# k by heads in 1 KB runs, v of the first two batches without its column of ones, q of the second batch in 768 B runs

## The chip, the cores and the metric

The kernel is one program on one core of a Trainium2 chip. A core has five engines with their own instruction streams: PE (TensorE, matrix products into eight PSUM banks; its weight loads are listed as PEld), DVE (VectorE), ACT (ScalarE), POOL (GpSimd) and SP (SyncE, which here only issues DMAs). Each works through its own list in order and waits on semaphores for the others. The metric is the device time of one execution in microseconds; of several executions the median is taken.

## The reference

```python
B, H, S, D = 8, 8, 576, 64                      # float32 q, k, v
q_s = exp(q - max(q, axis=-1));  q_s /= sum(q_s, axis=-1) + 1e-09     # over the 64 columns of a row
k_s = exp(k - max(k, axis=2));   k_s /= sum(k_s, axis=2) + 1e-09      # over the 576 rows of a head
kv  = einsum('bhsd,bhse->bhde', k_s, v)         # 64x64 per batch and head
att = einsum('bhsd,bhde->bhse', q_s, kv)        # -> x: 4608 tokens x 512
h   = x @ w_in                                  # 512 -> 2048, float64 weights
out = (h / (1 + exp(-1.702 * h)) @ w_out)       # 2048 -> 512, float32
```

The attention is linear: per batch and head a 64x64 matrix kv is built from k and v, and the softmaxed q is multiplied by it. Then comes a two-layer feed-forward network. The two weight matrices arrive as float64, 8.4 MB each; the kernel splits each into a high and a low float32 half, so that three products (high by high, high by low, low by high) stand for one.

## The kernel before, in words

The 4608 tokens are cut into 12 blocks t of 384 (a partition holds three neighbouring rows, C = 3). A batch has 576 rows, so block 0 lies in batch 0 and block 1 spans batches 0 and 1. The 2048 hidden columns are cut into 16 pieces j of 128. For every pair (t, j) there is `g1` (12 matmuls 128x384 on line 593: for each of four 128-row chunks c of x the products wh by xh, wh by xl, wl by xh), the gelu on ACT (`gt`), its high half on ACT (`gh`) and its low half on DVE (`gl`, line 605), and `g2` (three parts of three matmuls 128x512, line 625: gh by wh, gh by wl, gl by wh).

Weights are loaded once. `load_w` brings 512 KB of raw float64 per piece; `conv_w` makes the two halves in place: c1 on ACT (line 248), c2 on DVE (line 252), c3 on DVE (lines 256 and 257), c5 on ACT (line 261, the high half) and c6 on DVE (line 267, the low half). The word "wi3" below is the piece j = 3 of `w_in`, "wo3" of `w_out`.

The attention of the first two batches is done in groups of four heads (`group`), from buffers that sit in the memory which the late weights take over afterwards (`early`, with a tag per weight tile). k comes in 512 of its 576 rows (four neighbouring rows, CM = 4, per partition) and a tail of 64 rows (`load_tail`). Per group of four heads the steps are

- `k_max`: three maxima on DVE (lines 390 to 392), then a maximum over the partitions on POOL;
- `k_sub`: subtraction on DVE (lines 414, 417), exponential on ACT (lines 420, 421); of batch 0 the result goes to a second buffer `em` with the heads inside the chunks;
- `q_soft`: row maxima and subtraction on DVE (lines 493, 494), exponential on ACT (line 497), sums, reciprocals and the scaling on DVE (lines 500 to 503);
- `kv_pairs`, per pair of heads: for each of five row chunks and two heads one matmul (line 456) with k as the 64-column weights and v as the moving operand. v has a 65th column of ones, so the same matmul also gives the sum of k's exponentials; DVE turns that column into reciprocals r (lines 461, 462) and ACT scales with it (line 472);
- `q_tr`, three transposes per pair of heads on PE (line 520), copied to SBUF on ACT; `x_pairs`, the product with kv (lines 563, 568); and `x_out`, its high half xh on ACT (line 535) and low half xl on DVE (line 538).

Batches from 2 on go through the buffers kt, vt and qt in groups of two heads.

The order on every engine is set ahead of time: each step is put into `Plan` with an engine, an assumed cost, what it reads and writes, and a rank. `Plan.order` plays the steps through with these assumed costs, takes on each free engine the ready step of lowest rank, and so fixes the five lists. A load counts with a landing time worked out from its `size` at 270 KB/us. An engine keeps its list even if at run time a later step were ready first. Changing an assumed cost or a buffer therefore reorders lists far from the line that changed.

## Time and profile before

| | us |
|---|---|
| median of 3 runs (lowest, highest) | 917.77 (916.34, 918.44) |
| the profiled execution | 914.53 |
| its span, first to last instruction | 912.8 |
| PE busy in it | 880.8 |

A row of the timeline or of the chain of waits starts with a time from the span's start and a duration. The merged rows run from the first to the last instruction of a group. A row of the windows view gives for a stretch its length, then busy time and count of instructions of PE, PEld, DVE, ACT and POOL, the granted clock of PE, the share of the DMA engines and GB/s. PE is idle for 32 us in all, 12.1 of them before its first matmul. The DMA queue of SP is the only one that carries data.

### The profile page before, as it was taken

The page shows a single profiled execution, that of the slowest core. Times are in us where ns is not written, and L with a number is a line of the kernel's source. Part 1 is how long each engine was busy: PE and PEld are TensorE (multiplying, and loading weights), DVE is VectorE, ACT ScalarE, POOL GpSimd, SP SyncE. Part 2 cuts the span into 40 slices and gives each one's busy share as a digit, 9 for nine tenths or more (in the row PEclk, how much of TensorE's full clock was granted, in tenths as well). Part 3 has the DMA queues.
Part 4 walks back from the last instruction along what each step waited for, and adds up shares of the span by engine and source line. Part 5 has one row for each costly group of instructions (what it writes and reads, how often), then busy time and mean ns, then how long its engine had stood idle before and what let it go on. Part 6 is the DMA issues. An engine that isn't in the chain of part 4 may idle for free.

```text
span 912.8 us, 12680 instructions
## 1 busy us (share of the span) xinstructions
PE 880.8 (96%) x5040; PEld 778.0 (85%) x5040; DVE 388.8 (43%) x829; ACT 494.1 (54%) x844; POOL 25.1 (3%) x35
## 2 busy tenths in 40 slices
PE   2689999999999999999999999999999999999998
PEld 2479898888989888889889888889898888988996
DVE  8999994344522631331641452332263133131111
ACT  3776668456843972552872693553494365252222
POOL 1000001000100100000100000000010000000000
PEclk9899999999999999999999999999999999999999
DMA  9998000113300510000700510000241000100000
GB/s 234 276 377 247 3 1 1 53 52 74 65 35 18 113 36 18 18 10 35 122 18 35 112 29 36 18 18 36 47 90 38 14 14 20 33 10 1 35 1 34
DMA packets 124506, 55.34 MB, mean 61 GB/s; under 512 B 107552, under 2 KB 117792, under 8 KB 124448
## 3 DMA queue, kind: packets, MB, share of 16 engines
q1 hardware_dynamic: 124448, 54.54, 23.5%
q8 instruction: 39, 0.64, 0.3%
q14 instruction: 19, 0.16, 0.1%
HBM read 45.09 MB, written 9.44 MB: 60 GB/s over the span
## 4 chain that ended last, share of the span: by engine, by line
PE 94%; DVE 4%; ACT 1%; DMA 1%; issue 0%; SPq 0%; ACTq 0%; DVEq 0%
PE bank L593 44%; PE bank L625 44%; PE bank L456 2%; PE bank L520 2%; PE bank L568 2%; PE bank L563 1%; DMA ek<-in_k 1%; DVE eq L494 0%; DVE tmp L257 0%; DVE tmp L256 0%; DVE qm L493 0%; DVE qm L500 0%; DVE w L267 0%; DVE em L414 0%; DVE xl L538 0%
## 5 line engine op out<-in xcount | busy, mean ns | idle before, releaser
L593 PE MATMUL bank<-xh,w 128*128 128x384 f32 x1536 | 428.9, 340 | 2.1 <-ACT w L261 1.6
L625 PE MATMUL bank<-w,gh 128*128 128x512 f32 x1152 | 365.6, 398 | 1.4 <-ACT gh L602 1.4
L593 PEld LDWEIGHTS bank<-xh,w 128*128 128x128 f32 x1536 | 281.6, 188 | 14.0 <-issue 3.8
L605 DVE TENSOR_TENSOR gl<-g,gh 128x384 fp32r<-128x384 f32 x192 | 106.7, 556 | 383.2 <-ACT gh L602 382.9
L599 ACT ACTIVATE g<-bank 128x384 f32<-128x384 f32 x192 | 94.5, 492 | 323.3 <-PE bank L593 322.4
L593 PE MATMUL bank<-xl,w 128*128 128x384 f32 x768 | 259.7, 338 | 0.0
L625 PEld LDWEIGHTS bank<-w,gh 128*128 128x128 f32 x1152 | 213.8, 189 | 42.0 <-issue 5.0
L625 PE MATMUL bank<-w,gl 128*128 128x512 f32 x576 | 228.8, 397 | 3.1 <-DVE gl L605 3.0
L593 PEld LDWEIGHTS bank<-xl,w 128*128 128x128 f32 x768 | 144.3, 188 | 7.1 <-DVE xl L538 0.2
L625 PEld LDWEIGHTS bank<-w,gl 128*128 128x128 f32 x576 | 108.7, 189 | 29.9 <-DVE gl L605 4.0
L602 ACT CAST gh<-g 128x384 fp32r<-128x384 f32 x192 | 98.5, 513 | 6.0
L599 ACT ACT_TABLE_LOAD x56 | 71.8, 1283 | 1.0
L493 DVE TENSOR_REDUCE qm<-qt 128x6 f32<-128x384 f32 x40 | 22.1, 552 | 67.6 <-DMA qt<-in_q 67.2
L497 ACT ACT_TABLE_LOAD x35 | 44.9, 1283 | 1.2 <-DMA qt<-in_q 0.5
L396 POOL PARTITION_ALL_REDUCE mx<-mx x28 | 23.9, 855 | 646.3 <-DVE mx L392 646.3
L527 ACT COPY qT<-bank 128x384 f32<-128x384 f32 x48 | 22.7, 477 | 27.1 <-PE bank L520 26.9
L500 DVE TENSOR_REDUCE qm<-qt 128x6 f32<-128x384 f32 x40 | 22.0, 550 | 23.0 <-ACT qt L497 22.9
L420 ACT ACT_TABLE_LOAD x21 | 26.9, 1283 | 1.1 <-PEq L761 0.7
L538 DVE TENSOR_TENSOR xl<-bank,xh 128x384 fp32r<-128x384 f32 x48 | 24.7, 549 | 2.1 <-ACT xh L535 2.0
L472 ACT ACTIVATE kvn<-bank,r 64x64 f32<-64x64 f32 x64 | 17.9, 306 | 14.1 <-DVE r L462 12.2
L248 ACT ACTIVATE tmp<-raw 128x512 f32<-128x512 f32 x32 | 21.3, 677 | 7.2 <-DVE w L267 5.1
L494 DVE TENSOR_TENSOR qt<-qt,qm 128x384 f32<-128x384 f32 x40 | 22.3, 559 | 3.8 <-DVE qm L493 0.5
(72 smaller groups left out, 458.8 us busy)
## 6 DMA issues: line engine op xcount, KB each, us to landing
out<-tmp SPq DMA_DIRECT2D x36, 256.0 KB, 2.1
raw<-in_moe_w_in SPq DMA_DIRECT2D x16, 512.0 KB, 9.6
raw<-in_moe_w_out SPq DMA_DIRECT2D x16, 512.0 KB, 9.1
kt<-in_k SPq DMA_DIRECT2D x24, 256.0 KB, 4.4
vt<-in_v SPq DMA_DIRECT2D x48, 128.0 KB, 4.0
qt<-in_q SPq DMA_DIRECT2D x36, 96.0 KB, 2.6
qt<-in_q SPq DMA_DIRECT2D x16, 192.0 KB, 2.9
ek<-in_k SPq DMA_DIRECT2D x4, 512.0 KB, 5.7
```

The costliest lines, as they stand in the source:

```text
L396: nc.gpsimd.partition_all_reduce(flat, flat, P, bass_isa.ReduceOp.max)
L420: nc.scalar.activation(t, t, AF.Exp)
L493: nc.vector.tensor_reduce(out=m, in_=qt, axis=AX.X, op=ALU.max)
L494: nc.vector.tensor_tensor(out=qt, in0=qt, in1=bc(m, D), op=ALU.subtract)
L497: nc.scalar.activation(qt, qt, AF.Exp)
L527: nc.scalar.copy(qT, pq[:, :TB])
L538: nc.vector.tensor_tensor(out=xl, in0=px[:, :TB], in1=xh.bitcast(F32), op=ALU.subtract)
L593: nc.tensor.matmul(ph, wi[w][j][:, c, :], x[:, c, :], start=c == 0 and i == 0, stop=c == KC - 1 and i == 2,)
L599: nc.scalar.activation(gt, ph, AF.Gelu_apprx_sigmoid)
L602: nc.scalar.copy(gh, gt)
L605: nc.vector.tensor_tensor(out=gl, in0=gt, in1=gh.bitcast(F32), op=ALU.subtract)
L625: nc.tensor.matmul(po[c], x[:, cs], wo[w][j], start=j == 0 and i == 0, stop=j == NJ - 1 and i == 2)
```

## The change

k of every batch is now held with the heads outside and the four chunk rows inside, as it lies in memory: one run of 1 KB per partition and head instead of four of 256 B (batch 0 had that already, and then moved the data into `em`; this second buffer and the reordering are gone, `k_sub` works in place). v of batches 0 and 1 is loaded in runs of 1 KB too, one DMA per four heads instead of one per head; for that its column of ones is taken out, and `kv_pairs` of these batches makes a second round of matmuls for that column alone, with the same weights and a one-column tile `one` (for the tail, the ones that stand in `vl`). q of batch 1 is loaded in runs of 768 B as batch 0's was, and like it goes to a second buffer `en` in its last step; that buffer takes the tags wo10 and wo11, and wo5 and wo6, which `em` had, are free from the start. The planner's assumed costs follow: 0.5 us of SP instead of 2.4 for four heads of v, their size by 1 instead of 1.5, and 0.1 us more of PE for a pair of heads. The matmuls, the arithmetic and the results are otherwise as before. The lists of all engines change through the planner.

```diff
-    kt_ = [sb(f"kt{i}", [P, CM, 2, D]) for i in range(NP)]
+    kt_ = [sb(f"kt{i}", [P, 2, CM, D]) for i in range(NP)]
...
+    one = sb("one", [P, 1])
+    nc.vector.memset(one, 1.0)
...
         ek[0, gr] = early(f"wi{5 + gr}", f"ek0{gr}", [P, 4, CM, D], 0)
-        em[0, gr] = early(f"wo{5 + gr}", f"em0{gr}", [P, CM, 4, D], 0)
...
-        ev[0, gr] = early(f"w{'io'[gr]}9", f"ev0{gr}", [P, 4, CM, W], 0)
-        ek[1, gr] = early(f"wo{14 + gr}", f"ek1{gr}", [P, CM, 4, D], 1)
-        eq[1, gr] = early(f"wi{14 + gr}", f"eq1{gr}", [P, C, 4, D], 1)
-        ev[1, gr] = early(f"wo{12 + gr}", f"ev1{gr}", [P, 4, CM, W], 1)
-        for b in range(2):
-            nc.vector.memset(ev[b, gr][0][:, :, :, D:W], 1.0)
+        en[1, gr] = early(f"wo{10 + gr}", f"en1{gr}", [P, C, 4, D], 1)
+        ev[0, gr] = early(f"w{'io'[gr]}9", f"ev0{gr}", [P, 4, CM, D], 0)
+        ek[1, gr] = early(f"wo{14 + gr}", f"ek1{gr}", [P, 4, CM, D], 1)
+        eq[1, gr] = early(f"wi{14 + gr}", f"eq1{gr}", [P, 4, C, D], 1)
+        ev[1, gr] = early(f"wo{12 + gr}", f"ev1{gr}", [P, 4, CM, D], 1)
...
         def run():
+            if b < 2:
+                nc.sync.dma_start(
+                    out=t.rearrange("p h c d -> p h (c d)"),
+                    in_=v[b, n * i : n * (i + 1), 0:SM, :].rearrange("h (p c) d -> p h (c d)", c=CM),
+                )
+                return
             for h in range(n):
...
-        plan.add("SP", n * 0.6, (), (key,), rank, run, size=1.5 * n * SM * D * 4)
+        if b < 2:
+            plan.add("SP", plan.ISSUE, (), (key,), rank, run, size=n * SM * D * 4)
+        else:
+            plan.add("SP", n * 0.6, (), (key,), rank, run, size=1.5 * n * SM * D * 4)
...
-                    if t == 0:
+                    if t < 2:
                         nc.sync.dma_start(
                             out=qt[p0:p1].rearrange("p h c d -> p h (c d)"),
...
-        src, skey = t, key
-        if b == 0:
-            src = t.rearrange("p h c d -> p c h d")
-            t, key = kbuf[b, i] = em[b, i]
...
-                out=t, in0=src, in1=mx.unsqueeze(1).broadcast_to([P, CM, n, D]), op=ALU.subtract
+                out=t, in0=t, in1=mx.unsqueeze(2).broadcast_to([P, n, CM, D]), op=ALU.subtract
...
-                for c in range(CM + 1):
-                    for a in range(2):
-                        lhs = kt[:, c, o + a, :] if c < CM else kl[:, 2 * hp + a, :]
-                        rhs = vt[:, o + a, c, :] if c < CM else vl[:, 2 * hp + a, :]
...
+                for cols in (slice(0, D), slice(D, W)) if b < 2 else (slice(0, W),):
+                    for c in range(CM + 1):
+                        for a in range(2):
+                            lhs = kt[:, o + a, c, :] if c < CM else kl[:, 2 * hp + a, :]
+                            rhs = vt[:, o + a, c, :] if c < CM else vl[:, 2 * hp + a, cols]
+                            if cols.start == D:
+                                rhs = vl[:, 2 * hp + a, cols] if c == CM else one
...
-        plan.add("PE", 0.57 * len(hps) + 0.36, reads, (PB,), rank, run)
+        plan.add("PE", (0.57 + 0.1 * (b < 2)) * len(hps) + 0.36, reads, (PB,), rank, run)
...
-        if t == 0:
-            m = qm[i % 2].rearrange("p c h -> p (c h)").rearrange("p (h c) -> p h c", h=n)
+        dst, nkey = qt, key
+        if t < 2:
+            m = qm[i % 2].rearrange("p (h c) -> p h c", h=n)
             qn, nkey = qbuf[t, i] = en[t, i]
```

The lists at the three places that the prediction speaks of follow. Before means the list of the kernel before, after that of the changed kernel. The numbers in the names tell buffers apart.

The first place is PE's list in batch 0, from the transposes of the first four heads to the third pair of heads (`kv_pairs`, `ev01` is v, `em01` or `ek01` is k, `et` the tail). Before:

```order
L520 MATMUL bank1_62<-ident_69,en00_120 128x128 x3
L520 MATMUL bank3_64<-ident_69,en00_120 128x128 x3
L456 MATMUL bank0_61<-ev01_131,em01_128 64x65 x8
L456 MATMUL bank0_61<-et_137 64x65 x2
L563 MATMUL bank4_65<-qT0_96,kvn0_70 128x384
```

After:

```order
L524 MATMUL bank1_62<-ident_69,en00_121 128x128 x3
L524 MATMUL bank3_64<-ident_69,en00_121 128x128 x3
L460 MATMUL bank0_61<-ev01_131,ek01_127 64x64 x8
L460 MATMUL bank0_61<-et_135 64x64 x2
L460 MATMUL bank0_61<-one_117,ek01_127 64x1 x8
L460 MATMUL bank0_61<-et_135 64x1 x2
```

A pair has twenty matmuls instead of ten; the ten new ones have one moving column, and they stand ahead of the next step, the x product.

The second place is DVE's list around `gl1`, the low half of the very first gelu (L605 before, L609 after; `ek10` is k of batch 1's first four heads). Before:

```order
L414 TENSOR_TENSOR ek10_122<-ek10_122,mx1_101 128x1024
L417 TENSOR_TENSOR kl0_103<-kl0_103,mx1_101 64x256
L605 TENSOR_TENSOR gl1_82<-g1_77,gh1_81 128x384
L390 TENSOR_TENSOR m1_102<-ek11_132 128x512
L391 TENSOR_TENSOR mx0_100<-m1_102 128x256
```

After (`raw_177` is the raw wi1):

```order
L414 TENSOR_TENSOR ek10_124<-ek10_124,mx1_101 128x1024
L417 TENSOR_TENSOR kl0_103<-kl0_103,mx1_101 64x256
L252 TENSOR_SCALAR raw_177<-raw_177 128x512
L256 SCALAR_TENSOR_TENSOR tmp0_85<-tmp0_85,raw_177 128x512
L257 SCALAR_TENSOR_TENSOR tmp0_85<-raw_177,tmp0_85 128x512
L609 TENSOR_TENSOR gl1_82<-g1_77,gh1_81 128x384
```

Steps c2 and c3 of wi1 moved ahead of `gl1`; the maxima of batch 1's other four heads moved behind it.

The third place is DVE's list before the low half of wi3, on which `g1` of (0, 3) waits. Before (`raw_256` is wi3, `raw_269` wo3, `w_587` the low half of wo2, `w_604` that of wi3):

```order
L538 TENSOR_TENSOR xl1_75<-bank4_65,xh1_74 128x384
L538 TENSOR_TENSOR xl1_75<-bank5_66,xh1_74 128x384
L267 TENSOR_TENSOR w_587<-tmp0_85,w_587 128x512
L252 TENSOR_SCALAR raw_256<-raw_256 128x512
L256 SCALAR_TENSOR_TENSOR tmp1_86<-tmp1_86,raw_256 128x512
L257 SCALAR_TENSOR_TENSOR tmp1_86<-raw_256,tmp1_86 128x512
L605 TENSOR_TENSOR gl0_80<-g0_76,gh0_79 128x384
L252 TENSOR_SCALAR raw_269<-raw_269 128x512
L267 TENSOR_TENSOR w_604<-tmp1_86,w_604 128x512
```

After (`raw_193` is wi3, `raw_195` wo3, `w_661` the low half of wo2, `w_668` that of wi3):

```order
L252 TENSOR_SCALAR raw_193<-raw_193 128x512
L256 SCALAR_TENSOR_TENSOR tmp1_86<-tmp1_86,raw_193 128x512
L257 SCALAR_TENSOR_TENSOR tmp1_86<-raw_193,tmp1_86 128x512
L252 TENSOR_SCALAR raw_195<-raw_195 128x512
L256 SCALAR_TENSOR_TENSOR tmp2_87<-tmp2_87,raw_195 128x512
L257 SCALAR_TENSOR_TENSOR tmp2_87<-raw_195,tmp2_87 128x512
L542 TENSOR_TENSOR xl1_75<-bank4_65,xh1_74 128x384
L542 TENSOR_TENSOR xl1_75<-bank5_66,xh1_74 128x384
L267 TENSOR_TENSOR w_661<-tmp0_85,w_661 128x512
L267 TENSOR_TENSOR w_668<-tmp1_86,w_668 128x512
L609 TENSOR_TENSOR gl0_80<-g0_76,gh0_79 128x384
```

Before, only c2 of wo3 stood between c3 of wi3 and its low half, beside `gl0`; now both c2 and c3 of wo3 do, the last two low halves of x (`xl1`) and the low half of wo2, and `gl0` comes behind. On PE, all three parts of `g2` for (0, 2) now stand behind `g1` of (0, 3), where before two of them stood ahead of it.

## Prediction

> **What bounds the kernel now.** I read the windows by stage first, then who waits for whom in the first 62 us, then the chain of waits of that stretch. Columns of the windows: length, busy time of PE, PEld, DVE, ACT, POOL, granted clock, DMA share, GB/s.

> ```profile
> span 912.8 us, 12680 instructions
> ...
> 8.30:30.00 21.70, 12.16 (x110) 9.28 (x111) 20.02 (x39) 13.39 (x27) 2.41 (x3) 1.00 1.19 229
> 30.00:57.00 27.00, 17.12 (x134) 13.31 (x134) 25.97 (x51) 20.51 (x37) 2.13 (x2) 0.81 1.01 348
> 57.00:120.00 63.00, 62.90 (x317) 56.78 (x316) 59.18 (x106) 41.78 (x75) 0.00 (x0) 1.00 0.52 158
> ```

> From 57 us on PE is full, and the list of its waits over the whole span names none after that. Whatever the change does there off PE is hidden; it can pay only by letting PE enter its full stretch earlier. From 8 to 57 us PE is busy for 29.3 of 48.7 us. The DMA engines look full too, but DVE is busy for 46.0 of these 48.7. Which of the two is the bound is told by the waits.

> ```profile
> DVE m L390 <- DMA ek<-in_k: 1.8, 2, 1.1
> DVE w L267 <- ACT w L261: 0.9, 1, 0.9
> ACT tmp L248 <- DMA raw<-in_moe_w_in: 1.5, 1, 1.5
> ACT tmp L248 <- DMA raw<-in_moe_w_out: 0.5, 1, 0.5
> PE bank L520 <- DVE r L461: 4.8, 1, 4.8
> PE bank L520 <- DVE eq L503: 3.1, 1, 3.1
> PE bank L625 <- DVE gl L605: 3.0, 1, 3.0
> ```

> DVE waits for a transfer twice, both times for the first k (until 8.3 us), and those two loads are already in 1 KB runs. Afterwards DVE's only waits are short ones for ACT and PE. ACT waits 2.0 us for the raw weights wi1 and wo1, but DVE was still working on its earlier steps. The chain says the same (start, duration, what):

> ```profile
> 2.66 5.57 DMA ek<-in_k
> ...
> 20.91 1.28 PE bank L456 x20
> ...
> 24.38 0.73 PE bank L456 x20
> ...
> 28.85 0.93 DVE xl L538 x2
> ...
> 51.04 0.97 DVE eq L503
> 52.05 0.88 PE bank L520 x6
> ```

> After that first load no transfer stands on it. It runs through DVE's list, and in batch 0 through the third and fourth `kv_pairs` (20.91 and 24.38), because DVE's reciprocals wait for them. So the loads that the change shortens bound nothing, while the matmuls that it adds stand on the chain.

> **The transfers** do become faster:

> ```profile
> 7.00:10.00 3.00, 0.00 (x0) 0.00 (x0) 1.80 (x5) 0.00 (x0) 1.11 (x2) 1.00 1.11 328
> ...
> 23.00:28.00 5.00, 4.12 (x35) 2.44 (x33) 4.04 (x9) 4.05 (x10) 0.00 (x0) 1.00 1.36 186
> ...
> 37.77 0.68 ACT L248 ACTIVATE tmp<-raw 128x512 f32<-128x512 f32 x1 [1.48 <-DMA raw<-in_moe_w_in]
> ```

> In 7 to 10 us the queue carries runs of 768 B and 1 KB at 328 GB/s, in 23 to 28 us runs of 256 B at 186. From 10 us on there remain v of batch 0 (1.05 MB), wi0 and wo0 (1.05), batch 1 (3.15) and wi1 (0.52): 5.8 MB, at 328 GB/s 17.6 us, so wi1 lands near 29.5 us (with about 2 us for completion) instead of 37.8. Now DVE first wants it (c2 of wi1) near 36.5, as worked out below. I count the gain as 0 beyond ACT's 2.0 us, which DVE's work covers. The four memsets that go lie before the first k lands, and `em` was no extra instruction. The later loads of k, and the weights that change places with loads of block 2, are covered by DVE, which converts two pieces in about 5 us while the queue brings two in under 3.

> **The second round of matmuls.** Each of the eight pairs gets twenty more PE instructions in the trace (a pair shows as 20). No row shows a one-column matmul. Below the cost is bounded by 0, above by the pair as it stands: 1.28 us in the slow phase, 0.73 in the fast one. The twenty weight loads are the same and only the moving columns go from 65 to 1, so I take three quarters to four fifths: 0.95 and 0.6. The first two pairs are hidden in the 4.8 us for which PE then waits. The third and fourth are not:

> ```profile
> 22.31 0.16 DVE L461 TENSOR_SCALAR r<-bank 128x1 f32<-128x1 f32 x1 [0.23 <-PE bank L456]
> ...
> 25.29 0.15 DVE L461 TENSOR_SCALAR r<-bank 128x1 f32<-128x1 f32 x1
> ```

> DVE's first reciprocal goes from 22.31 to 23.26. The fourth pair's piece of the chain starts at 24.38 + 0.95 = 25.33 and ends at 25.33 + 0.73 + 0.6 = 26.7; the reciprocal that stood at 25.29 stands at 26.7: **1.4 us late**. With cost 0 it is 0, with the whole pairs 24.38 + 1.28 + 2 x 0.73 = 27.1, 1.8. Up to the row maxima of batch 1's q (31.82 below) DVE then does the same steps in another order: the wait of 0.9 for w falls away, one of like length for the x product of the fourth pair comes instead. So 1.4 stays. The four pairs of batch 1 lie in PE time that waits for DVE, see below.

> [...]

> **The order.** Prices of DVE's steps, start to next start:

> ```profile
> 30.30 0.69 DVE L390 TENSOR_TENSOR m<-ek 128x512 f32<-128x512 f32 x1
> ...
> 31.82 0.94 DVE L493 TENSOR_REDUCE qm<-eq 128x12 f32<-128x768 f32 x1
> ...
> 33.67 1.22 DVE L414 TENSOR_TENSOR ek<-ek,mx 128x1024 f32<-128x1024 f32 x1
> ...
> 35.14 0.54 DVE L605 TENSOR_TENSOR gl<-g,gh 128x384 fp32r<-128x384 f32 x1
> ...
> 37.12 0.94 DVE L500 TENSOR_REDUCE qm<-eq 128x12 f32<-128x768 f32 x1
> ...
> 39.55 0.42 DVE L252 TENSOR_SCALAR raw<-raw 128x512 uint32<-128x512 uint32 x1
> 40.07 0.70 DVE L256 SCALAR_TENSOR_TENSOR tmp<-tmp,raw 128x512 int32<-128x512 int32 x1
> ...
> 41.42 0.42 DVE L252 TENSOR_SCALAR raw<-raw 128x512 uint32<-128x512 uint32 x1
> ...
> 43.28 0.68 DVE L267 TENSOR_TENSOR w<-tmp,w 128x512 fp32r<-128x512 f32 x1
> 43.88 0.15 DVE L461 TENSOR_SCALAR r<-bank 128x1 f32<-128x1 f32 x1
> ...
> 44.15 0.67 DVE L267 TENSOR_TENSOR w<-tmp,w 128x512 fp32r<-128x512 f32 x1
> ```

> `k_max` 1.5, first half of `q_soft` 1.85, `k_sub` 1.47, gl 0.47 (taken as an xl, of the same shape), second half of `q_soft` 2.43, c2 0.5, c3 1.35, c6 0.6, reciprocals 0.27, xl 0.47 (two in 0.93 on the chain).

> First `gl`: q's maxima at 31.82 + 1.4 = 33.2, `k_sub` done 33.2 + 1.85 + 1.47 = 36.5, c2 and c3 of wi1 (new here) 38.4, `gl` done 38.9, where now it is at 35.7. PE's wait in `g2` grows by 3.2 us. That costs nothing yet: PE is ahead of DVE until the full stretch, and `g1` of (0, 1), which now waits for wi1, finds it ready.

> Then DVE goes on: `q_soft` 41.3, c6 of wi1 41.9, wo1 43.8, `k_max` 45.3, c6 45.9, two reciprocals 46.4, `q_soft` 48.3, `k_sub` 49.7, c2 and c3 of wi2 51.6, `q_soft` 54.0 (now 52.0; 1.4 late, and 0.6 net of steps drawn forward). Two xl 54.9, reciprocal 55.2, c6 of wi2 55.8, gl 56.3, reciprocal 56.5, c2 and c3 of wo2, wi3 and wo3 (3 x 1.85) 62.1, two xl 63.0, c6 of wo2 63.6, c6 of wi3 **64.2**. Now:

> ```profile
> 46.21 1.81 PE L563 MATMUL bank<-qT,kvn 128*128 128x192 f32 x8
> ...
> 61.79 0.69 DVE L267 TENSOR_TENSOR w<-tmp,w 128x512 fp32r<-128x512 f32 x1
> ...
> 62.59 0.34 PE L593 MATMUL bank<-xh,w 128*128 128x384 f32 x1
> ...
> 64.70 0.62 PE L625 MATMUL bank<-w,gh 128*128 128x512 f32 x2
> ...
> 65.44 0.44 PE L593 MATMUL bank<-xh,w 128*128 128x384 f32 x1
> ```

> `g1` of (0, 3) now starts at 62.59 and lasts 2.11; one third of `g2` (0.7) later, at 65.44, `g1` of (1, 0) starts, and from there to the end PE has the same work in both kernels. PE reaches that place early this time: from 54.0 it has two transposes, the fourth pair of batch 1 with its second round (1.33), `g1` of (0, 2) 2.11, two x products (1.81 by the row) and three thirds of `g2`, done near 62.2. So c6 of wi3 sets the time: the third of twelve matmuls starts at about 64.3, ten of them (1.76) end at 66.1, three thirds of `g2` (2.1) at 68.2 instead of one. 68.2 - 65.44 = **2.75 us later**: 1.4 from the second round, 1.35 from DVE's and PE's new order.

> Span 912.8 + 2.75 = 915.55, the profiled execution 914.53 + 2.75 = 917.3. That execution lies 3.2 us below the median, so the median goes to 917.77 + 2.75 = **920.5 us**.

> **The rivals.** *The second round is nearly free.* The lateness of 1.4 us falls away, the order's 1.35 stays: 919.1. For it: PE's time for dense matmuls goes with the columns (0.73 us for 65 columns, two heads side by side, against 0.88 for six transposes of 128). Against it: the weight loads stay.

> *The loads were the bound, and the kernel gets faster.* If ACT's waits for wi1 and wo1 hold up DVE behind the page's back, their 2.0 us come back, the new order is as good as the old and the second round hides: 915.8. It decides as soon as a step of DVE in 30 to 57 us starts earlier because wi1 or wo1 lies there earlier. Against it: DVE's waits name no transfer after 8.3 us.

> *The long wait cools PE.* PE's wait ahead of `gl` grows from 3.0 to about 6 us and another of 2 us stands before `g1` of (0, 3).

> ```profile
> 50.00:55.00 5.00, 2.95 (x31) 2.71 (x31) 4.83 (x11) 4.62 (x10) 0.00 (x0) 0.86 1.06 382
> 55.00:60.00 5.00, 5.00 (x23) 4.62 (x23) 4.30 (x9) 2.55 (x5) 0.00 (x0) 0.80 1.06 375
> ```

> Here the clock was 0.5 for (0.14 + 0.20) x 5 / 0.5 = 3.4 us after a wait of 3.1. Before 62 us the 2 us that PE has in hand absorb that. After the wait before `g1` of (0, 3) nothing does: half of 3.4, 1.7 us more, 922.2. [...]

> *Longer runs are no faster.* wi1 lands at 37.8 as now, its c3 starts after ACT's c1 at 38.5 instead of 37.0, and everything behind it is 1.4 later: 921.9. Against it: 328 against 186 GB/s.

> **How the numbers follow.** This kernel's measurement tells about 0.2% (1.84 us) from no change; the bounds are 915.9 and 919.6. Forecast 0.48, nearly free 0.27, cooled PE 0.13, loads as bound 0.08, runs no faster 0.04. Slower by over 0.2% is the forecast without its lower edge (0.43), and the cooled PE and slow runs (0.17): 0.60. Within: the rest, 0.32. Faster: 0.08. The forecast's own range is 919.1 (second round free) to 920.9 (whole pairs, 1.8 - 1.4 more), plus 0.5 for waits of ACT that I left out. With the cooled PE above and half of the ground towards the faster case below: 917.5 to 923.0.

> **What would show it.** Right: one-column matmuls of 20 to 45 ns from start to start; DVE's reciprocal of the fourth pair near 26.7 us; `gl` ending near 38.9; PE waiting for the low half of wi3 until about 64.3; wi1 in the chain nowhere; PE full from there. Wrong: a second round of under 0.2 us, a transfer in DVE's waits after 9 us, or `g1` of (1, 0) starting before 66.

## The result, and the profile after

| | before | after |
|---|---|---|
| median, us | 917.56 | 922.79 |
| executions (lowest, highest) | 4 (916.34, 918.44) | 4 (921.67, 923.71) |
| profiled execution, its span | 914.53, 912.8 | 923.71, 921.9 |
| PE busy in it | 880.8 | 892.5 |

The changed kernel is slower: ratio 1.0065, 95% interval 1.0052 to 1.0079, by the medians 5.2 us. The forecast was 920.5, that is 2.75 more than before: the sign is right and the size about half of what came. The two profiles lie 9.1 us apart in span, because the one of before is faster than its four timed executions and the one of after is the slowest of its own.

The windows by stage of the changed kernel (columns as in the prediction):

```profile
8.30:30.00 21.70, 15.15 (x177) 12.83 (x178) 17.22 (x33) 10.71 (x21) 2.41 (x3) 1.00 1.11 308
30.00:57.00 27.00, 17.59 (x137) 13.16 (x137) 23.77 (x43) 18.67 (x32) 3.01 (x2) 0.86 1.03 330
57.00:120.00 63.00, 61.95 (x359) 55.89 (x356) 57.40 (x105) 42.78 (x80) 0.00 (x0) 0.92 0.44 137
```

The transfers did become faster (308 GB/s against 229 in the first stretch). But DVE's busy time there fell from 20.02 to 17.22 us: it now waits. Who waits for whom up to 76 us (total, times, longest):

```profile
DVE r L465 <- PE bank L460: 4.6, 3, 1.8
DVE xl L542 <- ACT xh L539: 4.3, 4, 1.7
DVE m L394 <- DMA ek<-in_k: 1.7, 1, 1.7
...
PE bank L629 <- DVE gl L609: 3.5, 1, 3.5
```

The same waits of the kernel before:

```profile
DVE xl L538 <- ACT xh L535: 0.6, 1, 0.6
...
DVE r L461 <- PE bank L456: 0.2, 1, 0.2
```

DVE's wait for PE's pairs was 0.2 us and is 4.6, that for xh (which waits for PE's x product) was 0.6 and is 4.3. PE has become the bound of a part in which DVE was it. PE's timeline shows why; start, duration, operation, merged rows of the changed kernel:

```profile
13.06 0.45 PE L460 MATMUL bank<-et 128*64 128x64 f32 x4
13.27 0.99 PE L460 MATMUL bank<-one,ek 128*64 128x1 f32 x16
14.09 0.39 PE L460 MATMUL bank<-et 128*64 128x1 f32 x4
...
19.29 1.51 PE L524 MATMUL bank<-ident,en 128*128 128x128 f32 x6 [2.68 <-DVE r L465]
...
21.85 0.96 PE L460 MATMUL bank<-one,ek 128*64 128x1 f32 x16
...
22.96 2.92 PE L567 MATMUL bank<-qT,kvn 128*128 128x384 f32 x4
25.68 0.85 PE L524 MATMUL bank<-ident,en 128*128 128x128 f32 x3
26.45 1.12 PE L460 MATMUL bank<-ev,ek 128*64 128x64 f32 x16
...
27.58 0.96 PE L460 MATMUL bank<-one,ek 128*64 128x1 f32 x16
28.40 0.36 PE L460 MATMUL bank<-et 128*64 128x1 f32 x4
28.69 0.90 PE L524 MATMUL bank<-ident,en 128*128 128x128 f32 x3
...
31.97 1.65 PE L567 MATMUL bank<-qT,kvn 128*128 128x384 f32 x2 [1.10 <-ACT kvn L476]
...
36.25 0.34 PE L597 MATMUL bank<-xl,w 128*128 128x384 f32 x1
```

And the rows of the kernel before at the same steps:

```profile
22.12 1.93 PE L563 MATMUL bank<-qT,kvn 128*128 128x384 f32 x4
23.89 0.49 PE L520 MATMUL bank<-ident,en 128*128 128x128 f32 x3
24.30 0.69 PE L456 MATMUL bank<-ev,em 128*64 128x65 f32 x16
```

A one-column pass (the twenty matmuls of one second round) starts at 13.27 and the next pair at 14.30: 1.03 us for the pass, where the 64-column pass ahead of it took 1.09 (12.18 to 13.27). That is not the larger loss. After the x products, four matmuls in 2.92 us, three transposes take 0.85 and the fourth pair's first sixteen matmuls 1.12; before, the same took 1.93, 0.49 and 0.69. PE has been busy since 19.29 but runs at half speed, and it goes on so, with one wait of 1.10 us at 30.9, until about 35.7 us. (The granted-clock column reads 1.00 in this stretch in both kernels and does not show it; the durations do.)

### The profile page after: what moved, and what is told of

It is laid out like the page before. It is cut to its first block, busy times and chain, and to the rows that moved or that the text cites. A ratio compares the mean times of both kernels' runs of the same rounds, so it can differ in the third digit from the quotient of the medians.

```text
span 921.9 us, 13008 instructions
## 1 busy us (share of the span) xinstructions
PE 892.5 (97%) x5200; PEld 788.3 (86%) x5200; DVE 390.2 (42%) x826; ACT 498.7 (54%) x848; POOL 26.8 (3%) x35
## 4 chain that ended last, share of the span: by engine, by line
PE 96%; DVE 2%; ACT 1%; DMA 1%; SPq 0%; issue 0%; ACTq 0%; DVEq 0%
PE bank L597 44%; PE bank L629 44%; PE bank L460 3%; PE bank L524 2%; PE bank L572 2%; PE bank L567 1%; DMA ek<-in_k 1%; DVE ek L414 0%; DVE eq L498 0%; DVE qm L497 0%; DVE w L267 0%; ACT kvn L476 0%; ACT xh L539 0%; DVE m L394 0%; ACT L501 0%
## 5 line engine op out<-in xcount | busy, mean ns | idle before, releaser
L609 DVE TENSOR_TENSOR gl<-g,gh 128x384 fp32r<-128x384 f32 x192 | 106.7, 556 | 384.1 <-ACT gh L606 383.8
L629 PEld LDWEIGHTS bank<-w,gl 128*128 128x128 f32 x576 | 108.6, 189 | 29.5 <-DVE gl L609 3.9
L539 ACT CAST xh<-bank 128x384 fp32r<-128x384 f32 x48 | 20.9, 478 | 7.4 <-PE bank L567 6.9
L248 ACT ACTIVATE tmp<-raw 128x512 f32<-128x512 f32 x32 | 21.0, 671 | 6.7 <-DVE w L267 6.7
```

The lines of the kernel that those rows point to most:

```text
L609: nc.vector.tensor_tensor(out=gl, in0=gt, in1=gh.bitcast(F32), op=ALU.subtract)
L629: nc.tensor.matmul(po[c], x[:, cs], wo[w][j], start=j == 0 and i == 0, stop=j == NJ - 1 and i == 2)
```

## Experiments

All comparisons with the kernel before are on the same chip; us are (ratio - 1) x 917.3. Two readings of the profile serve throughout: when the first output transfer is issued (the loss ahead of it is that of the first stage), and how long a block of 384 rows takes where PE is full, from one output transfer to the next; this time per block is called the pace. In the last column the pace is taken out: 10.16 blocks (that much follows the first output) times the difference from 73.31. The first output is read from one execution and moves with it: in those of e2 and e7, for instance, DVE had the second k at 9.27 and 9.31 us instead of 8.15, so both stand about 1.1 us later for that alone.

| run | ratio (95% interval) | us | first output | block | us without pace |
|---|---|---|---|---|---|
| before, twice (e5) | | | 168.19, 170.48 | 73.31 | 0 |
| after | 1.0065 (1.0052, 1.0079) | +6.0 | 178.26 | 73.24 | +6.7 |
| e1 before, split | 1.0073 (1.0057, 1.0090) | +6.7 | 176.72 | 73.30 | +6.8 |
| e2 after, no second round | 1.0000 (0.9991, 1.0010) | 0.0 | 172.27 | 73.25 | +0.6 |
| e3 second round 64 wide | 1.0040 (1.0025, 1.0055) | +3.7 | 172.32 | 73.38 | +3.0 |
| e4 v as before | 0.9975 (0.9965, 0.9985) | -2.3 | 169.13 | 73.17 | -0.9 |
| e6 e4 in the new order | 1.0001 (0.9991, 1.0010) | +0.1 | 172.23 | 73.17 | +1.5 |
| e7 second round 16 wide | 1.0032 (1.0020, 1.0043) | +2.9 | 178.37 | 73.03 | +5.8 |
| e8 k alone | 0.9980 (0.9971, 0.9989) | -1.8 | 170.93 | 73.17 | -0.4 |
| e9 before with a spare tile | 0.9964 (0.9952, 0.9976) | -3.3 | 170.59 | 72.99 | -0.1 |
| e10 e4 with a spare tile | 0.9955 (0.9940, 0.9969) | -4.1 | 169.46 | 72.97 | -0.7 |
| e11 e4, idle places filled | 0.9965 (0.9953, 0.9977) | -3.2 | 168.06 | 73.17 | -1.8 |
| e12 after, idle places filled | 1.0001 (0.9987, 1.0016) | +0.1 | 174.40 | 73.25 | +0.7 |
| e13 e4, both | 0.9943 (0.9928, 0.9957) | -5.2 | 167.75 | 72.96 | -1.7 |

**e1: the second round alone, in the old order.**

```diff
+for cols in (slice(0, D), slice(D, W)) if b < 2 else (slice(0, W),):
     for c in range(CM + 1):
...
-        rhs = vt[:, o + a, c, :] if c < CM else vl[:, 2 * hp + a, :]
+        rhs = vt[:, o + a, c, cols] if c < CM else vl[:, 2 * hp + a, cols]
```

> The kernel before, with one change: for the first two batches the 65 columns of a pair's product are taken as 64 and then 1, from the same tile, so ten one-column matmuls per pair are added and the order of all other work, the layouts and the transfers stay. Theory T (the one-column matmuls take as long as those with 64 columns, 1.03 to 1.11 us a pair at half clock and 0.63 at full, and beside that do not count as work for TensorE's clock, so that it stays at half speed for one or two 3.4 us stretches longer): 4 to 6 us over the kernel before, 921.5 to 923.5. Rival D (only their duration on the way to the reciprocals counts): 1.5 to 2.0 over, 919.0 to 919.6. Rival O (the new order of the DVE list is what costs): within 0.5 of the kernel before.

923.09 us (922.86 to 925.49): the whole loss, without any other part of the change. D and O fall as the main cause. The 3.4 us in T are how long the clock stood at half in the kernel before, 53.6 to 57.0 us (0.62 in the half microsecond from 53.5, 0.50 from 54.0 to 57.0, 0.96 in the next half); that the clock moves in such stretches was an assumption.

**e2: the changed kernel without it.**

```diff
-for cols in (slice(0, D), slice(D, W)) if b < 2 else (slice(0, W),):
+for cols in (slice(0, D),) if b < 2 else (slice(0, W),):
...
-nc.vector.tensor_scalar_add(r, pk[:, :, D], 1e-9)
+nc.vector.tensor_scalar_add(r, pk[:, :, 0 if b < 2 else D], 1e-9)
```

> The changed kernel without the second round: the ones column's matmuls of the first two batches are left out and the reciprocal reads column 0 of the product instead, so the normalisation of these two batches is not computed; the planner's prices, and with them every list, stay those of the changed kernel. Theory T: the loss goes back to what the new order costs, 0 to 1.4 us over the kernel before, 917.5 to 919. Rival D: 2 us under the changed kernel, 920.5 to 921. Rival O: within 0.7 of the changed kernel, 922 to 923.

This kernel leaves out the sums of k's exponentials for the two batches and takes another column in their place; its other work and its lists are those of the changed kernel. 917.29: nothing is left of the loss. The second round costs 6.0 us here and 6.7 in the old order.

**e3: as many matmuls, but wider.**

```diff
-one = sb("one", [P, 1])
+one = sb("one", [P, D])
...
+dst = bank[bk][r0 : r0 + D, 2 * P : 2 * P + D] if cols.start == D else pk[r0 : r0 + D, m, cols]
```

> The changed kernel with the second round of matmuls 64 columns wide instead of 1: the ones are 64 columns, written into a spare part of the bank; the count of instructions and every list stay. It gives TensorE more to do in the same places. Theory T (narrow matmuls do not count for the clock): TensorE comes to full speed one stretch earlier, 2 to 4 us under the changed kernel, 919 to 921. Rival D: no faster, 922.5 to 923.5 (the same count of matmuls of about the same length). Rival O: the same as the changed kernel within 0.5.

920.79, 2.0 under the changed kernel (2.3 by the ratios, with an interval of about 1.9 to either side), although the second round has 64 times the columns. Its PE timeline:

```profile
14.18 1.09 PE L461 MATMUL bank<-ev,ek 128*64 128x64 f32 x16
15.04 0.37 PE L461 MATMUL bank<-et 128*64 128x64 f32 x4
15.22 0.64 PE L461 MATMUL bank<-one,ek 128*64 128x64 f32 x16
...
22.53 1.56 PE L568 MATMUL bank<-qT,kvn 128*128 128x384 f32 x4
23.93 0.49 PE L525 MATMUL bank<-ident,en 128*128 128x128 f32 x3
24.35 0.69 PE L461 MATMUL bank<-ev,ek 128*64 128x64 f32 x16
```

PE is at full speed inside the second pair already (1.09 us for sixteen matmuls, then 0.64), 3 us after its first matmul at 12.02, and again from 22.3, 3.1 us after it resumed at 19.15. With one column it needed 16 us. The order and the count are the same and the width differs, so the width is taken as the reason; that the moment at which the two executions were caught had no part in it was not shown.

**e7: 16 columns.** As e3, with `one` and its place in the bank 16 wide.

> The changed kernel with the second round 16 columns wide: between the one column of the change (922.8) and the 64 columns of e3 (920.8). The lists and the count of instructions stay. If width counts in proportion, 16 columns are still too little for TensorE's clock and the time is that of the changed kernel, 922.3 to 923.3; if any matmul that is not a single column counts, it is that of e3, 920.3 to 921.3.

920.16, which by the expectation's words would speak for "any matmul that is not a single column counts". The profile, of the slowest of its seven executions, says otherwise: the first output comes at 178.37, and without the 1.2 us of the late k still at 177.2, nearly as late as with one column, and the time is made good by a faster pace later (73.03). Without the pace the loss is 5.8, between one column (6.7) and 64 (3.0), and within the interval of the former. What width would have been enough stays open.

**e4, e8, e6: the transfers and the order.** e4 gives v its column of ones, its 256 B runs and the planner's old prices back, and k and q stay in long runs; DVE, ACT and PE then have the order of before. e8 takes q's runs back too. e6 is e4 with the changed kernel's prices, and so its order.

```diff
-ev[0, gr] = early(f"w{'io'[gr]}9", f"ev0{gr}", [P, 4, CM, D], 0)
+ev[0, gr] = early(f"w{'io'[gr]}9", f"ev0{gr}", [P, 4, CM, W], 0)
...
-plan.add("PE", (0.57 + 0.1 * (b < 2)) * len(hps) + 0.36, reads, (PB,), rank, run)
+plan.add("PE", 0.57 * len(hps) + 0.36, reads, (PB,), rank, run)
```

> The changed kernel with v of the first two batches as before (64 columns and the ones beside them in the tile, 256 B runs, the planner's prices for v and for the pairs as before, no second round); k in 1 KB runs and q of the second batch in 768 B runs stay. The order on DVE, ACT and PE is that of the kernel before. Theory T: 0 to 1 us under the kernel before (the transfers are not the bound, one or two waits of DVE for k go), 916.5 to 917.5. Rival O: the same. Rival L (shorter transfers do help, and the second round alone spoils it): 1.5 to 2.5 under, 915 to 916.

> The kernel of e4 with q of the second batch as before, in 256 B runs: k in 1 KB runs alone (in every batch). If the 2.2 us that e4 gained over the kernel before come from k's transfers, 914.6 to 915.8; if q's 768 B runs carry them, 916.5 to 917.5.

> The kernel of e4 (k and q in long runs, v as before, no second round) with the planner's new prices, so that every list stands as in the changed kernel: the new order alone. If the order costs what the forecast gave it, 1.0 to 2.5 us over e4, 916.1 to 917.6, and v's longer runs are worth about nothing (the kernel without the second round had 917.3). If the order is free, within 0.5 of e4's 915.1, and v's longer runs would then cost 2, which no row speaks for.

915.12, 915.49 and 916.78. The first looked like rival L (shorter transfers help): 2.3 us. But 1.4 of it lies in the pace, and what remains in the first stage is 0.9 +- 0.9. e8 does not tell k's part from q's. The new order costs e6 - e4 = 2.4 +- 1.3 us at the same pace; v's longer runs (e2 against e6) are worth 0.9 +- 1.3 without the pace, so nothing that can be told.

**e5: the kernel before once more.**

> The kernel before, unchanged, for a second profile: its first profiled execution (914.53 us) was faster than every timed one (915.41 to 919.42). If the part before TensorE is full without a break differs from execution to execution (the clock comes back a stretch sooner or later), the first layer's step that started at 65.4 us starts 1 to 3 us later here and the span is longer by as much; if the difference lies elsewhere, it starts within 0.3 us of 65.4.

916.85, span 915.1. The first layer's step that stood at 65.44 stands at 67.73, and the first output at 170.48 instead of 168.19: all 2.3 us of difference lie ahead of PE's full stretch.

```profile
22.19 2.75 PE L563 MATMUL bank<-qT,kvn 128*128 128x384 f32 x4
...
45.98 0.84 PE L593 MATMUL bank<-xh,w 128*128 128x384 f32 x2
```

The x products took 2.75 us instead of 1.93 and `g1` of (0, 1) ran at half speed (0.84 for two matmuls, 0.51 in the first profile): the same lists, the clock granted at other moments. All executions of this kernel lie between 914.3 and 919.4 us, so this accounts for a part of its scatter; the rest was not traced.

**e9, e10: the place of the tiles.** The blocks of 73.31, 73.24, 73.17 and 73.03 us went with which tiles a kernel declares. e9 puts one unused tile of 64 B a partition into the kernel before; e10 widens the unused `one` of e4 from 4 to 64 B.

```diff
+pad = sb("pad", [P, 16])
+nc.vector.memset(pad, 1.0)
```

> The kernel before with one more tile of 16 columns (64 B a partition) that nothing reads, where the changed kernel has its ones column: every tile behind it, the weights among them, lies 64 B further on. A block of the part in which TensorE is full (one output transfer to the one 384 rows on, such as 483.80 to 557.11 us) took 73.31 us in both profiles of the kernel before and in e1, 73.24 in the changed kernel and e2, 73.17 in e4, e6 and e8, 73.38 in e3 and 73.03 in e7; these groups differ in where their tiles lie. Theory P (the place of the tiles sets this pace): a block other than 73.31 by 0.05 or more, and by ten blocks' worth of it a time other than the kernel before's, between 914 and 918.5; the first output transfer stays at 168 to 171. Rival (something in the changed code sets it, for instance k's layout): 73.30 to 73.32 and 916.5 to 917.5.

> The kernel of e4 with its unused ones column 16 columns wide, so that the tiles behind it lie 32 B further on; nothing else. Theory P: a block other than the 73.17 of e4, and by ten times the difference another time than its 915.1; 73.03, the shortest seen, would give 913.2 to 914. Rival: 73.17 and 914.6 to 915.6.

913.69 and 912.85. Output transfers of the kernel before, then of e9:

```profile
483.80 1.53 SPq L641 DMA_DIRECT2D out<-tmp  x3
557.11 1.54 SPq L641 DMA_DIRECT2D out<-tmp  x3
```

```profile
484.87 1.54 SPq L644 DMA_DIRECT2D out<-tmp  x3
557.86 1.54 SPq L644 DMA_DIRECT2D out<-tmp  x3
```

73.31 and 72.99 us for the same matmuls on a full PE: 0.4% of the kernel's time from a tile that nothing reads. Theory P holds (e9's 913.69 and e10's 72.97 go a little further than was expected), and with the pace taken out e9 is the kernel before (-0.1) and e10 is e4 (-0.7 and -0.9). The pace does not go with the chip: e4, e6 and e11 ran on three chips and all have 73.17.

**e11: the clock held up in e4.** Matmuls that nothing reads, in four places where PE waits. The first three read zeros; the fourth reads a tile that holds batch 0's kv by then:

```diff
+def heat(n, bk, z=1):
+    w = kvn[z].rearrange("p a b -> p (a b)")
+    for _ in range(n):
+        nc.tensor.matmul(bank[bk][:, 0:256], w[:, 0:P], w[:, 0:256], start=True, stop=True)
...
+            if (b, hps) == (0, (1,)):
+                heat(8, 7)
```

> The kernel of e4 with matmuls of 256 columns on zeros put into TensorE's idle places (16 before the first pair, 8 behind the second, 5 behind the first two of the first down projection, 5 behind the seventh pair), into a bank that is free then; no list changes otherwise. They keep TensorE's clock up where the kernel let it fall. If the clock costs time on the way in e4 too (DVE waits 0.9 for pairs and 1.2 for x there, and TensorE ran 3 us of the step at 44.08 at half speed), 1 to 3 us under e4, 912 to 914. If DVE alone bounds that part, within 0.5 of e4's 915.1, and if the added matmuls get in the way, over 915.6.

913.66, by the ratios 0.9 +- 1.4 under e4, so the times do not show a gain. In the profile the half-speed steps are gone up to 43 us, and so is DVE's wait for pairs; DVE's own list sets most of what remains.

**e12: the clock held up in the changed kernel.** The same four fills (the second with 5 and the third with 8 matmuls, the fourth ahead of the seventh pair), the second round kept.

> The changed kernel, its second round of one-column matmuls kept, with 256-column matmuls on zeros in four idle places of TensorE (16 ahead of the first pair, 5 behind the second, 8 behind the first two of the first down projection, 5 ahead of the seventh pair), into a free bank; no tile moves, all other lists stay. Theory T in its last form: of the 6.0 us that the second round costs, 2.3 are its duration and 3.7 the clock that it keeps low; work that does nothing but hold the clock up then makes the kernel faster by 2 to 4 us, 918.5 to 920.8, with the first output transfer at 173 to 176 instead of 178.3. Rival D (duration and order alone): no faster, 922.3 to 923.5, first output at 177.5 to 178.5.

917.50 (914.19 to 919.87): by the ratios 5.9 +- 1.8 us come back by adding work to an engine that was the bound. Theory T expected 2 to 4, D none. The profiled execution is the slowest of the twelve, and shows what the fills cannot hold:

```profile
19.58 0.85 PE L535 MATMUL bank<-ident,en 128*128 128x128 f32 x6 [2.26 <-DVE r L476]
20.48 0.69 PE L468 MATMUL bank<-ev,ek 128*64 128x64 f32 x16
...
22.04 2.93 PE L578 MATMUL bank<-qT,kvn 128*128 128x384 f32 x4
...
26.65 0.96 PE L468 MATMUL bank<-one,ek 128*64 128x1 f32 x16
...
35.03 0.52 PE L608 MATMUL bank<-xh,w 128*128 128x384 f32 x2
```

PE is at full speed at 19.58 (0.85 for six transposes), falls to half about 21.3 after the idle 2.26 us and then, busy without a break to 29.9, with two one-column passes in it, does not recover before about 35.

**e13: e11 with the spare tile of e10.**

> The kernel of e11 (k and q in long runs, v as before, the filled idle places) with the unused tile of e10: the three gains together. If they add up: 2.5 us (pace, e10 under e4 by the ratios 0.9955 and 0.9975 gives 1.8) and 0.9 to 1.5 (e11 under e4) under e4's 915.1, so 911.0 to 912.5.

911.24 (910.27 to 912.90), ratio 0.9943 (0.9928 to 0.9957): -5.2 us, where e11 has -3.2 and the pace gives -2.0 more. The gains add up, and this kernel is faster than the kernel before and than the changed one.

## Why the prediction was right or wrong

**The bound.** Right: in the kernel before DVE's list set the first stage, and after the first k no transfer bounded it. The raw wi1 is issued at 20.19 us instead of 32.29 now and ACT's waits for raw weights are gone, but nothing was gained by it that could be told: e4, k and q in long runs, is 0.9 +- 0.9 us faster in that stage. "I count the gain as 0" held within that. The 2 us allowed for a transfer's completion agree with the smallest loads of the kernel before: 48 KB of q landed 2.2 us after its issue (median of 24).

**The order.** Forecast 1.35 us, measured 2.4 +- 1.3 (e6 against e4). The changed kernel without the second round stands at +0.6: the order's cost, less what the longer runs give back (0.9 for k with q, 0.9 for v, neither beyond its interval). The term was good to about 1 us.

**The second round's own duration.** Its reason was wrong and its size came out by luck. In the changed kernel's first pair the pass of one column took 1.03 us and that of 64 1.09; at half speed the former is 1.03 to 1.11, where three quarters of a pair, 0.95, were taken. But the 1.28 us of the old pair held more than its pass, which took 1.14 where another pair followed (12.14 to 13.28), so the pair grew by 0.95 all the same (20.73 to 22.96 against 20.84 to 22.12), and at full speed by 0.52 (47.64 to 48.90 against 24.30 to 25.04), where 0.6 was forecast. DVE's reciprocal of the third pair came at 23.15 (forecast 23.26).

**The step that failed** is "the fourth pair's piece of the chain starts at 24.38 + 0.95 = 25.33 and ends at 25.33 + 0.73 + 0.6 = 26.7". It took the fourth pair and its second round at full clock, and by starting from 24.38 also the x products and transposes ahead of them, because the rows of before were at full clock. The changed kernel's rows:

```profile
23.15 0.16 DVE L465 TENSOR_SCALAR r<-bank 128x1 f32<-128x1 f32 x1 [1.18 <-PE bank L460]
...
28.80 0.16 DVE L465 TENSOR_SCALAR r<-bank 128x1 f32<-128x1 f32 x1 [1.81 <-PE bank L460]
...
31.42 0.56 DVE L542 TENSOR_TENSOR xl<-bank,xh 128x384 fp32r<-128x384 f32 x1 [1.67 <-ACT xh L539]
...
41.93 0.55 DVE L609 TENSOR_TENSOR gl<-g,gh 128x384 fp32r<-128x384 f32 x1
```

28.80 instead of 26.7: the pair started at 26.45 instead of 25.33, behind x products of 2.92 us against 1.93 and transposes of 0.85 against 0.49, and took 2.24 us (26.45 to 28.69) instead of 1.33. Behind it the x product at half speed made DVE wait 1.67, where 0.9 was forecast; `gl` ends at 42.48 instead of 38.9, 3.6 late. The second loss of this kind follows where PE resumed after a wait for ACT:

```profile
56.64 1.12 PE L460 MATMUL bank<-ev,ek 128*64 128x64 f32 x16 [2.18 <-ACT ek L420]
...
64.66 0.84 PE L597 MATMUL bank<-xh,w 128*128 128x384 f32 x2
...
75.75 0.34 PE L597 MATMUL bank<-xh,w 128*128 128x384 f32 x1
```

Half speed from 56.3 to about 66.5, where before it was 3.4 us (53.6 to 57.0). `g1` of (1, 0) starts at 75.75 instead of the forecast 68.2. Not all of these 7.5 us are the loss, as the two profiled executions lie 9.1 us apart and the medians 5.2.

Of the signs that the forecast named, no transfer stood in DVE's waits after 9 us and wi1 nowhere in the chain, as said; PE still waited for the low half of wi3, but until 71.79 instead of 64.3. The one-column matmuls took 51 to 55 ns from start to start at half speed (twenty in 1.03 to 1.11 us) and 31 at full (46.54 to 47.17), where 20 to 45 was named.

So the term "1.4 from the second round" measured 6.1 (after against e2, pace taken out). e3 splits it: with 64 columns, and the clock that these give, 2.4 are left, which is duration, and 3.7 are the clock. e12 puts the clock's share higher: with the fills 0.1 is left over e2, and if the fills alone are worth 0.9, as e11 against e4 has it without showing it, the duration is worth 1.0. So 3.7 to 5 us are the clock, each figure good to 1.5 to 1.9 us by the intervals of the two runs in it; the 1.4 that was forecast is about the duration alone.

**The rival that came nearest** was "the long wait cools PE" (chance 0.13, +1.7). It had the right resource, but looked for the loss after waits alone, and took 3.4 us of half speed after each. What it missed is that PE was busy from 56.64 on and yet at half speed until 66.5, 10.2 us after the clock fell at 56.3. No length of wait that lowers the clock was found: half speed followed waits of 2.18 us (changed kernel, 56.64) and 2.19 (e3, 52.67), full speed one of 2.24 (e3, 33.22: two matmuls 128x512 in 0.72, at half speed 1.05).

**"Longer runs are no faster", "nearly free", "the loads were the bound"** all fell, by 308 GB/s, by 1.03 us a pass and by the 0.9 us of e4, where 2.0 should have come.

**The pace** stood in no term: the lists after 57 us were "the same work in both kernels". The work was the same, and yet 0.07 us per block shorter, 0.7 us in all. Tiles had moved, which e9 and e10 make the likely reason; it was not tried in this kernel. It hid a part of the loss.

## What to carry to other kernels

In this kernel a matmul's price had two parts: its time, the same within a tenth for 1 and 64 columns (the two passes of the changed kernel's first pair, 1.03 and 1.09 us), and the clock at which the work behind it ran. Narrow matmuls in a stretch that started at half speed cost more by the second than by the first (3.7 to 5 us against 1.0 to 2.4), and a column of ones in the moving operand (a pass of 1.14 us instead of 1.09) was far cheaper than a round of its own (1.03 more). When a step is costed from a row at full clock, ask whether the changed stream would still run at that clock at that place (here four x products took 2.92 us instead of 1.93). Before a difference of half a per cent is put down to an edit, compare the pace of a stretch that the edit should not touch: one unread tile of 64 B made a block 72.99 us instead of 73.31 (e9).

## What the runs showed of the hardware

The granted-clock column reads 1.00 up to the first fall that it shows, at half-speed steps too, and is read from there on. Rows of the changed kernel, then of e3 (columns as above, the clock third from the end):

```profile
39.00:42.00 3.00, 0.02 (x1) 0.00 (x0) 2.86 (x6) 1.95 (x3) 0.00 (x0) 0.53 1.02 381
42.00:46.00 4.00, 3.47 (x11) 2.34 (x13) 3.86 (x9) 3.01 (x5) 0.00 (x0) 0.50 1.09 349
46.00:50.00 4.00, 4.00 (x89) 3.80 (x90) 3.77 (x11) 2.37 (x4) 1.19 (x1) 1.00 1.10 314
```

```profile
15.00:19.00 4.00, 0.99 (x30) 0.85 (x26) 3.86 (x7) 2.83 (x5) 0.00 (x0) 0.95 1.15 298
19.00:22.00 3.00, 2.85 (x32) 2.55 (x34) 2.66 (x9) 2.19 (x6) 0.00 (x0) 0.50 1.12 262
22.00:26.00 4.00, 4.00 (x70) 3.12 (x67) 3.13 (x9) 2.43 (x6) 0.00 (x0) 1.00 1.11 288
```

So the clock falls at 39.2 (0.53 over 3 us) and comes back at 46.0 in the one, falls at 18.6 (0.95 over 4 us) and comes back at 22.0 in the other: 6.8 us at half in the one, 3.4 in the other. The two kernels start their first pairs (12.18 and 12.02) and transposes (19.29 and 19.15) alike. Behind the first pair's 64 columns the changed kernel ran a one-column pass of 1.03 us (13.27 to 14.30) and the second pair at half speed (1.13 for sixteen matmuls, then 0.99); e3 ran a 64-column pass of 1.06 (13.12 to 14.18) and was at full speed within the second pair (1.09, then 0.64). Behind the transposes it was the same: full speed from 22.0 in e3, from 35.7 in the changed kernel. That the width made this difference is the reading that fits both kernels and e12's fills; how the clock is decided was not shown.

A limit of width is not found. With 16 columns (e7) the loss without the pace was 5.8 us, between 6.7 with one and 3.0 with 64.

**One unread tile changed the pace of a full TensorE.** Blocks of the same matmuls took 72.96 to 73.38 us in these kernels, and the two profiles of the kernel before agree to 0.01. One unread tile of 64 B took it from 73.31 to 72.99. Why the place matters, and for which tiles (weights, x, or what other engines touch meanwhile), was not tried.
